# First token block of a mixture with plain products, its combined weights made one block later, and its weights taken through three stages

## The chip, the core and the metric

The kernel runs on one NeuronCore of a Trainium2 chip. The metric is the device time of one launch in microseconds (us). Five instruction streams run side by side and meet through semaphores: TensorE (PE: matrix products), ScalarE (ACT), VectorE (DVE), GpSimd (POOL) and SyncE (SP), which here does nothing but start DMA transfers between HBM and the on-chip memory SBUF. Products add up in PSUM, in banks of 512 float32 per partition. Each engine takes its instructions strictly in the order of the program, so an instruction that waits holds up all behind it.

## What is computed

```python
attn = softmax(q @ k.T / 8 + min(bias of s, 0), causal) @ v      # 4 x 8 heads, 576 tokens, 64 wide
x    = attn, heads side by side                                  # 2304 x 512
h    = x @ w_in ;  x  = (h * sigmoid(1.702 * h)) @ w_out         # first mixture, 512 -> 2048 -> 512
h2   = x @ w2_in;  r  = maximum(h2, 0)
out  = (s * r * r + b) @ w2_out                                  # second mixture, 512 -> 2048 -> 512
```

The weights arrive as 64-bit floats. The result must be as good as float32, so every factor is split into a high part that the fast matrix format holds exactly and a low rest, and every product is done three times (low times high, high times low, high times high).

## The kernel before

Attention and the first mixture run interleaved up to about 608 us of the trace. Then `first_whole` does the last 256 tokens of the first mixture on its own (to 648.6 us). The second mixture follows in `second`, for three blocks of 768 tokens (block 0, 1, 2).

A block is two halves of 384 tokens (N2). Its 16 hidden groups of 128 columns (f) are taken two at a time, in 8 steps p. Viewed over two token halves, two hidden groups and two halves of the 512 inputs, a step is a 2x2 by 2x2 block product, and `second` forms it from 7 products instead of 8, after Winograd: some factors are sums or differences of blocks. Each of the 7 slots of a step (`PRODUCTS`) has 6 matmuls of 128x384 into one of the PSUM sums p, q, r (L713), which ACT and DVE take out and add (`taken`, `added`), square, scale and split into g2 (`squared`, `affine`, `high`, `low`; the `low` of the odd group runs on POOL). Between the slots, `y_next` gives PE the output products of an earlier step from the list `todo`, 5 or 6 matmuls of 128x512 (L729) a slot.

The combined weights are made once, in block 0, one step ahead: `sums_of` forms four sums on POOL (L613), `parts_of` splits a part into high and low on ACT and DVE (L629, L630), 4 parts a step, and `hold` and `release` store them to HBM (`parts_d`). Blocks 1 and 2 read them back.

The raw weights come through a ring. `fetch_next` starts a transfer of 512 KB on SP into one of the `RING` buffers, 4 of them; it may run ahead of the last finished weight by that many. `sign_w` (ACT, L139), `merge_w` (two DVE instructions, L149 and L151) make float32 of the 64 bits, `split_w` (ACT L159, DVE L160) splits the output weights `wo`. `first_beside` deals these out by hand over the 7 slots. The order of every instruction on every engine is the order of the code here (`manual_schedule`).

```python
WHOLE, PARTS, SUMS, DIFFS = (0, 1, 11), (3, 4, 5, 8, 9, 10), 2, (6, 7)
EARLY2, RING = 4, (12, 13, 14, 15)
if k < EARLY2 or k < min(len(order), n_split[0] + len(RING)):    # fetch_next
```

Of the kernel before, what the change touches and what calls it, by code (L numbers as in the profile page):

```python
# [17 lines left out]
P = 128  # L18
# [17 lines left out]
HALF2, LAG2 = 384, 4  # L36
EARLY2, RING = 4, (12, 13, 14, 15)
WHOLE, PARTS, SUMS, DIFFS = (0, 1, 11), (3, 4, 5, 8, 9, 10), 2, (6, 7)
# [31 lines left out]
def fused_kernel(ctx: ExitStack, tc: tile.TileContext, qkT, vP, s, w1i, w1o, w2i, w2o, s2, b2, out):  # L70
# [473 lines left out]
    parts_d = dram.tile([NP, 4, P, 4 * W], F32, name="parts_d")  # L544
    tail1, early = ExitStack(), ExitStack()
# [3 lines left out]
    order = [("wi", f) for f in range(EARLY2)]  # L549
    for f in range(0, NF, 2):  # L550
        order += [("wi", f + k) for k in (EARLY2, EARLY2 + 1) if f + k < NF] + [("wo", f), ("wo", f + 1)]
    came, n_signed, joined, n_split = [], [0], [], [0]
    whole, wo2 = {}, {}

    def fetch_next():
        k = len(came)
        if k < EARLY2 or k < min(len(order), n_split[0] + len(RING)):
            tag, f = order[k]
            place = (early_pool, f"raw{k}", 1) if k < EARLY2 else (wp, f"wi{RING[k % len(RING)]}", 1)
            came.append(fetch_w(place, w2i if tag == "wi" else w2o, f))  # L560

    def sign_next():
        if n_signed[0] < len(came):
            sign_w(came[n_signed[0]])
            n_signed[0] += 1

    def merge_next():
        k = len(joined)
        if k < n_signed[0]:
            tag, f = order[k]  # L570
# [5 lines left out]
            joined.append(merge_w(came[k], to))  # L576

    def join_next():
        sign_next()
        merge_next()  # L580

    def split_next():

        if n_split[0] < len(joined):
            tag, f = order[n_split[0]]
            if tag == "wo":
                wo2[f] = split_w(joined[n_split[0]], "wo", f)
            n_split[0] += 1
# [14 lines left out]


# [11 lines left out]
    def parts_of(p, k, first):  # L616
# [5 lines left out]
        if not first:  # L622
            nc.sync.dma_start(flat, kept)
            return
        if k in (1, 2):
            src = sums[p][:, 2 * k - 2 : 2 * k].rearrange("p a n -> p (a n)")
        else:
            src = whole[p][:, 0, :] if k == 0 else whole[p][:, 1, W:]
# [4 lines left out]
    class Tokens:  # L633
# [25 lines left out]
        def split(self, kind, i, engine):  # L659
            t = self.d[i, kind] if len(kind) == 1 else self.at(i, int(kind[0]) - 1, int(kind[1]) - 1)  # L660
            x = self.x[kind, i] = xs_pool[0].tile([P, 2, N2], F32R, tag=f"x{kind}{i}", name="xs")
# [10 lines left out]
    def first_whole(ui, joins):  # L672
# [20 lines left out]
        for f in range(NF):  # L693
            for _ in h_item(ui, f, x, join_next if f in joins else None):
                pass
# [22 lines left out]
    y_sums = {}  # L718
    Y_OUT = (*RING, *WHOLE)
    y_tags = ["y4", "y0", "y1", "y2", "y3", None]  # L720

    def y_of(block, p, g2):

        def one(t, k):
            if p == 0 and k == 0:
                pool, tag = (psY, y_tags[t]) if y_tags[t] else (psM, "m")
                y_sums[t] = pool.tile([P, C], F32, tag=tag, name="py2", bufs=1 if y_tags[t] else 3)
            f, (a, b) = 1 - k // 3, ((1, 0), (0, 1), (0, 0))[k % 3]
            nc.tensor.matmul(  # L729
                y_sums[t], g2[f][:, a, t * P : (t + 1) * P], wo2[2 * p + f][:, b, :],  # L730
                start=(p == 0 and k == 0), stop=(p == NP - 1 and k == 5),
            )
            if p == NP - 1 and k == 5:
                y_out(block, t, y_sums[t])

        todo.extend((one, t, k) for t in range(T2) for k in range(6))

    def y_out(block, t, sums):
        row = block * 2 * N2 + t * P
        y = wp.tile([P, 2 * CM], F32, tag=f"wi{Y_OUT[t % (3 if block < N_BLOCKS - 1 else T2)]}", name="y2")[:, :C]  # L740
# [15 lines left out]
    def second(pool, gates, block, x, before, beside):  # L756
# [7 lines left out]
        def squared(c):  # L764
            nc.vector.scalar_tensor_tensor(out=c, in0=c, scalar=0.0, in1=c, op0=ALU.max, op1=ALU.mult)  # L765

        def affine(c):
            nc.scalar.activation(c, c, AF.Identity, scale=s_sb, bias=b_sb)  # L768

        def high(c, g2, f):  # L770
            g2[f] = gates().tile([P, 2, 2 * N2], F32R, tag="g2", name="g2", bufs=5)
            nc.scalar.activation(g2[f][:, 0, :], c, AF.Copy)  # L772

        def low(c, g2, f, engine):
            engine.tensor_tensor(g2[f][:, 1, :], c, f32(g2[f][:, 0, :]), ALU.subtract)  # L775

        for p in range(NP):
            step = block * NP + p
# [4 lines left out]
            for slot, (bank, _, _, _) in enumerate(PRODUCTS):  # L783
# [29 lines left out]
                if step == 0:  # L813
                    y_next(0 if slot == 6 else 2 * NC)
                elif step > 1 or slot >= LAG2:
                    y_next(6 if slot == 4 else 5)
            y_of(block, p, g2)
        return before

    def first_beside(p, slot):  # L820

        if p + 1 < NP:
            if p > 0 and slot == 0:
                sums_of(p + 1)
            k = {1: 0, 2: 1, 4: 2, 5: 3}.get(slot)
            if k is not None and (p > 0 or k > 1):
                parts_of(p + 1, k, True)
        if slot in (0, 1, 3, 4):
            sign_next()
        if slot in (1, 3, 5, 6):  # L830
            merge_next()
        if slot in (2, 3, 4, 6):
            split_next()
        fetch_next()
        fetch_next()
# [17 lines left out]

    with tc.manual_schedule(engines={PE, ACT, DVE, POOL, SP}):
        tokens = [Tokens(b * 2 * N2, (WHOLE[0], WHOLE[1], WHOLE[2], SUMS) if b else None) for b in range(N_BLOCKS)]
        x = tokens[0]
        X_FIRST = {
            6: lambda: (x.split("11", 0, L), x.split("11", 1, L), x.diff(0, 0, D)),
            7: lambda: (x.split("2", 0, D), x.split("1", 0, D), x.split("21", 0, L)),
            8: lambda: (x.diff(0, 1, D), x.split("3", 0, D), x.split("21", 1, L)),  # L860
            9: lambda: (x.split("4", 0, D), x.diff(1, 0, D), x.split("22", 0, L)),
            10: lambda: (x.split("2", 1, D), x.split("1", 1, D), x.split("22", 1, L)),
            11: lambda: x.diff(1, 1, D),
            12: lambda: (x.split("3", 1, D), x.split("4", 1, D)),
        }
        for f in first_whole(len(units) - 1, range(2, 2 + EARLY2)):
# [8 lines left out]
            split_next()  # L875
            release()
            if f == 1 + EARLY2:
# [4 lines left out]
            if f in (4, 7):  # L882
                sums_of(0 if f == 4 else 1)
            if f in (4, 5, 6, 8):
                parts_of(0, (4, 5, 6, 8).index(f), True)
            elif f in (11, 13):
                parts_of(1, (11, 13).index(f), True)
            if f >= RING[0]:
                fetch_next()
            if f in X_FIRST:  # L890
                X_FIRST[f]()
        tail1.close()
        pool = ctx.enter_context(tc.tile_pool(name="second", bufs=1, reuse_waits="tile"))
        before, gate_pool = [], []

        def gates():
            if not gate_pool:
                release(True)
                mixing.close()
                gate_pool.append(ctx.enter_context(tc.tile_pool(name="gates", bufs=1, side="right", reuse_waits="tile")))  # L900
            return gate_pool[0]
# [67 lines left out]
```

## Time and profile before

| | |
|---|---|
| time, median of 3 runs (lowest to highest) | 1065.11 us (1062.91 to 1065.68) |
| the profiled execution: its time, its span | 1064.85 us, 1063.1 us |
| PE busy | 1008.9 us (95%) |
| DVE busy | 681.5 us (64%) |
| ACT busy | 588.7 us (55%) |
| POOL busy | 365.2 us (34%) |
| mean granted clock of PE | 0.99 of 2.4 GHz |

The span is the stretch from the first to the last instruction that the profiler recorded. Busy shares are means over stages that differ: the page's slices show PE busy to nine tenths or more nearly everywhere, and to seven and eight tenths in a few slices between 664 and 771 us.

### The profile page before, as it was taken

How to read it: one execution, taken by the hardware profiler on the slowest of the kernel's cores; microseconds unless marked ns; L12 is line 12 of the kernel's file. 1: busy time of each engine (PE TensorE's matmuls, PEld its weight loads, DVE VectorE, ACT ScalarE, POOL GpSimd, SP SyncE). 2: the span in 40 equal slices, each digit the busy share in tenths (PEclk: the TensorE clock that was granted, in tenths of full speed). 3: DMA queues.
4: the chain of work that ended last, by engine and by line, in shares of the span. 5: the costliest groups of instructions: out<-in, count | busy, mean ns of one | idle time of the engine just before them, and what ended most of it. 6: DMA issues, size and time to landing. Idle time of an engine off the chain costs nothing. (4 is left out here: it accounts for less than half of the span.)

```text
span 1063.1 us, 17668 instructions
## 1 busy us (share of the span) xinstructions
PE 1008.9 (95%) x6264; PEld 921.1 (87%) x6264; DVE 681.5 (64%) x1453; ACT 588.7 (55%) x1322; POOL 365.2 (34%) x392
## 2 busy tenths in 40 slices
PE   5989999999999999999999999789899999999998
PEld 3459989999989999999999999677778888888887
DVE  5689877566467788878887476778884223642232
ACT  4788856646536646656656455645554342543332
POOL 2116535435335445435444282423321110310110
PEclk9998999999999999999999999999999999999999
DMA  6665432221042222222221146466754334342321
GB/s 193 197 222 185 123 99 56 64 81 44 11 133 71 69 92 70 83 90 82 77 86 51 46 183 208 134 221 210 238 216 160 130 119 158 138 173 96 139 70 60
DMA packets 51856, 129.58 MB, mean 122 GB/s; under 512 B 7068, under 2 KB 17432, under 8 KB 51768
## 3 DMA queue, kind: packets, MB, share of 16 engines
q1 hardware_dynamic: 51560, 128.32, 36.8%
q8 instruction: 50, 0.82, 0.3%
q14 instruction: 38, 0.31, 0.1%
q10 hardware_dynamic: 208, 0.13, 0.0%
HBM read 99.65 MB, written 24.71 MB: 117 GB/s over the span
## 5 line engine op out<-in xcount | busy, mean ns | idle before, releaser
L416 PE MATMUL ph<-xT,wi 128*128 128x320 f32 (+1 forms) x1536 | 245.8, 305 | 6.0 <-ACT xT L402 2.5
L729 PE MATMUL py<-wo,g 128*128 128x512 f32 x864 | 230.3, 398 | 11.0 <-DVE wo L160 11.0
L416 PEld LDWEIGHTS ph<-xT,wi 128*128 128x128 f32 x1536 | 216.6, 192 | 7.8 <-ACT xT L402 3.0
L456 PE MATMUL py<-g,wo 128*128 128x320 f32 (+1 forms) x1344 | 215.5, 304 | 0.0
L729 PEld LDWEIGHTS py<-wo,g 128*128 128x128 f32 x864 | 160.7, 189 | 39.1 <-DVE wo L160 13.1
L456 PEld LDWEIGHTS py<-g,wo 128*128 128x128 f32 x1344 | 188.2, 189 | 0.9
L443 POOL TENSOR_TENSOR g<-th,g 128x320 fp32r<-128x320 f32 (+1 forms) x128 | 111.7, 874 | 121.8 <-ACT g L442 120.1
L775 POOL TENSOR_TENSOR g<-odd,g 128x768 fp32r<-128x768 f32 x24 | 47.6, 1984 | 303.9 <-ACT g L772 303.9
L301 ACT ACTIVATE x<-x,m 64x64 f32<-64x64 f32 (+2 forms) x160 | 89.4, 559 | 99.5 <-DVE m L295 97.9
L713 PE MATMUL sum_p<-xs,part 128*128 128x384 f32 x576 | 119.7, 343 | 4.0 <-ACT e L759 4.0
L713 PEld LDWEIGHTS sum_p<-xs,part 128*128 128x128 f32 x576 | 105.1, 192 | 14.1 <-ACT e L759 6.5
L269 POOL TENSOR_TENSOR lo<-raw,hi 64x576 fp32r<-64x576 f32 (+1 forms) x56 | 68.2, 1218 | 123.3 <-PE ps L289 54.1
L295 DVE CUSTOM_DVE_ANT_0 x<-ps,mask 64x64 f32<-64x64 f32 (+2 forms) x160 | 68.1, 426 | 52.1 <-PE ps L289 50.2
L327 PE MATMUL pst<-ident,x 128*128 128x128 f32 (+2 forms) x480 | 85.9, 287 | 10.0 <-DVE ph L336 8.6
L759 ACT ACTIVATE e<-sum_p 128x384 f32<-128x384 f32 x72 | 35.2, 489 | 97.5 <-PE sum_p L713 97.5
L116 POOL TENSOR_SCALAR x<-x,tot 64x64 f32<-64x64 f32 (+1 forms) x96 | 49.4, 522 | 93.0 <-DVE tot L306 54.7
L333 ACT ACTIVATE ph<-pst 64x256 fp32r<-64x256 f32 (+2 forms) x144 | 67.1, 474 | 20.7 <-PE pst L327 19.3
L442 ACT ACTIVATE g<-th 128x320 fp32r<-128x320 f32 (+1 forms) x128 | 56.4, 441 | 40.1 <-DVE th L438 39.6
L327 PEld LDWEIGHTS pst<-ident,x 128*128 128x128 f32 (+2 forms) x480 | 54.9, 136 | 24.9 <-DVE ph L336 13.2
L437 ACT ACTIVATE th<-ph 128x320 f32<-128x320 f32 (+1 forms) x128 | 51.5, 402 | 35.5 <-PE ph L416 33.6
L438 DVE SCALAR_TENSOR_TENSOR th<-th,ph 128x320 f32<-128x320 f32 (+1 forms) x128 | 57.3, 448 | 20.9 <-ACT th L437 19.8
L118 DVE TENSOR_SCALAR hi<-raw 128x832 fp32r<-128x832 f32 (+1 forms) x48 | 69.0, 1437 | 2.3 <-DMA raw<-qkT 2.1
(100 smaller groups left out, 1607.9 us busy)
## 6 DMA issues: line engine op xcount, KB each, us to landing
part<-parts_d SPq DMA_DIRECT2D x48, 512.0 KB
raw<-qkT SPq DMA_DIRECT2D x32, 416.0 KB
parts_d<-part SPq DMA_DIRECT2D x24, 512.0 KB
pair<-w1o SPq DMA_DIRECT2D x16, 512.0 KB
pair<-w1i SPq DMA_DIRECT2D x16, 512.0 KB
pair<-w2i SPq DMA_DIRECT2D x16, 512.0 KB
pair<-w2o SPq DMA_DIRECT2D x16, 512.0 KB
raw<-qkT SPq DMA_DIRECT2D x24, 320.0 KB
```

Of the source, the lines that this page charges most:

```text
L118: nc.vector.tensor_scalar(out=out, in0=in_, scalar1=scale, scalar2=None, op0=ALU.mult)
L269: nc.gpsimd.tensor_tensor(lo[:D, kc], raw[:D, kc], f32(hi[:D, kc]), ALU.subtract)
L295: nc.vector.tensor_tensor_reduce(out=x[:w, j0:j1], in0=ps[:w, : j1 - j0], in1=mask[:w, WIDE - a0 + j0 : WIDE - a0 + j1], scale=-1.0 / ROOT ...
L301: nc.scalar.activation(x[:w, :a1], x[:w, :a1], AF.Exp, bias=least, scale=-1.0, accum_out=tot[:w, c : c + 1])
L327: nc.tensor.transpose(ps[: j1 - j0, at : at + a1 - a0], t["x"][c][: a1 - a0, j0:j1], ident[: a1 - a0, : a1 - a0])
L333: nc.scalar.activation(t["ph"][:rows, base:end], ps[:rows, :m], AF.Copy)
L416: nc.tensor.matmul(ph[:, :n], wi[f][:, a, cc * P : (cc + 1) * P], x[cc][:, b, :n], start=(k == 0), stop=(k == 3 * NC - 1),)
L438: nc.vector.scalar_tensor_tensor(out=th[:, :n], in0=th[:, :n], scalar=1.0, in1=ph[:, :n], op0=ALU.add, op1=ALU.mult)
L443: nc.gpsimd.tensor_tensor(g[:, 1, :n], th[:, :n], f32(g[:, 0, :n]), ALU.subtract)
L456: nc.tensor.matmul(py[:, :n], wo[f][:, a, wc], g_t[ui, f][:, b, :n], start=(k == 0), stop=(k == 3 * G - 1))
L713: nc.tensor.matmul(ps[:, :N2], w[:, a, c0 : c0 + P], x[kind, k // 3][:, b, :], start=(first and k == 0), stop=(k == 5), skip_group_check=n ...
L729: nc.tensor.matmul(y_sums[t], g2[f][:, a, t * P : (t + 1) * P], wo2[2 * p + f][:, b, :], start=(p == 0 and k == 0), stop=(p == NP - 1 and ...
```

## The change

Block 0 leaves `second` and gets a loop of its own, `halves`. It goes through 16 groups f times 2 token halves, 32 slots, 4 to a step of two groups. A slot has 12 matmuls of 128x384 with the split weights of one group themselves (`wi2`, the plain product, no combinations), then up to 8 output products; ACT takes the sum out with one copy, and after the second half the group is squared, scaled and split. The output products of a group are listed as soon as the group is done, not two groups at a time.

The raw ring gets 8 buffers. `weight_next`, once a slot, does three things for three different weights: it merges the next one, splits the one merged a slot before, and signs the one after. The split of an input weight is used by `halves` directly; as the first and the fourth part of the Winograd form are just pieces of it, those are stored to `parts_d` from there, and the merged float32 weights are stored too (`whole_d`).

Block 1 now makes the other two parts: it reads the merged weights back (`fetch_whole`), forms the sums on POOL and splits two parts a step, storing them for block 2; the other two it reads. The splits of block 0's tokens need 8 pieces and no differences; those of block 1 move to the last steps of block 0 (`X_SECOND`).

```diff
-EARLY2, RING = 4, (12, 13, 14, 15)
-WHOLE, PARTS, SUMS, DIFFS = (0, 1, 11), (3, 4, 5, 8, 9, 10), 2, (6, 7)
+EARLY2, RING = 4, (8, 9, 10, 11, 12, 13, 14, 15)
+WHOLE, SPLIT = (0, 1), (2, 3, 4, 5, 6, 7)
+PARTS, SUMS, DIFFS = (12, 8, 9, 3, 10, 4), 2, (6, 7)
...
+    def weight_next():
+
+        k = n_done[0]
+        ready = k < len(merged)
+        if len(merged) < n_signed[0]:
...
+            merged.append(merge_w(came[len(merged)], to))
+            if tag == "wi" and f % 2:
+                hold(1, whole_d[f // 2], whole[f // 2].rearrange("p f n -> p (f n)"))
+        if ready:
+            tag, f = order[k]
             if tag == "wo":
-                wo2[f] = split_w(joined[n_split[0]], "wo", f)
-            n_split[0] += 1
+                wo2[f] = split_w(merged[k], "wo", f)
+            else:
+                split_wi(f)
+            n_done[0] += 1
+        if n_signed[0] < len(came):
+            sign_w(came[n_signed[0]])
+            n_signed[0] += 1
...
+    def fetch_whole(p):
+        whole[p] = wp.tile([P, 2, CM], F32, tag=f"wi{WHOLE[0]}", name="whole")
+        nc.sync.dma_start(whole[p].rearrange("p f n -> p (f n)"), whole_d[p])
...
-        if not first:
+        if not first or k in (0, 3):
             nc.sync.dma_start(flat, kept)
             return
...
+        for s in range(4 * NP):
+            p, f, n = s // 4, s // 2, s % 2
...
+            for k in range(3 * NC):
+                cc, (a, b) = k // 3, ((1, 0), (0, 1), (0, 0))[k % 3]
+                nc.tensor.matmul(
+                    ps[:, :N2], wi2[f][:, a, cc * P : (cc + 1) * P], x[f"{cc // 2 + 1}{n + 1}", cc % 2][:, b, :],
+                    start=(k == 0), stop=(k == 3 * NC - 1),
+                )
+            beside(p, s % 4)
+            if s != 2:
+                y_next(6 * NC if s < 2 else 8)
+            nc.scalar.activation(c[:, n * N2 : (n + 1) * N2], ps[:, :N2], AF.Copy)
+            if n == 0:
+                continue
+            squared(c)
+            affine(c)
+            high(c, g2, f % 2)
+            low(c, g2, f % 2, nc.gpsimd if f % 2 and f > 1 else nc.vector)
+            if f < NF - 2:
+                y_of(0, (f,), g2)
...
+            if slot < 2 or 2 * p + slot + EARLY2 < NF:
+                weight_next()
+            release()
+            fetch_next()
+            fetch_next()
...
+                if block == 1 and p + 1 < NP:
+                    if slot == 1:
+                        sums_of(p + 1)
+                        if p + 2 < NP:
+                            fetch_whole(p + 2)
```

The order of the instructions shows three places. In the rows, `pair` is a raw weight, `pair<-pair` its signing, `wo` and `wi` split weights, `whole` a merged one, `part` a part of the Winograd form, `e`, `even`, `odd` and `c` sums taken out of PSUM. First ACT, from the first slot of a step in the middle of block 0, before:

```order
L759 ACTIVATE e<-sum_p 128x384
L768 ACTIVATE even<-even,b_sb,s_sb 128x768
L139 ACTIVATE pair<-pair 128x512
L772 ACTIVATE g_9221<-even 128x768
L629 ACTIVATE part<-whole 128x512
L139 ACTIVATE pair<-pair 128x512
L759 ACTIVATE e<-sum_p 128x384
L629 ACTIVATE part<-sums 128x512
L159 ACTIVATE wo_9246<-pair 128x512
L139 ACTIVATE pair<-pair 128x512
L759 ACTIVATE e<-sum_p 128x384
L629 ACTIVATE part<-sums 128x512
```

and the same place now, ACT from the first slot of a step in `halves`:

```order
L161 ACTIVATE wo_9063<-pair 128x512
L141 ACTIVATE pair<-pair 128x512
L810 ACTIVATE c<-ph_9048 128x384
L161 ACTIVATE wo_9095<-pair 128x512
L141 ACTIVATE pair<-pair 128x512
L810 ACTIVATE c<-ph_9079 128x384
L783 ACTIVATE c<-c,b_sb,s_sb 128x768
L787 ACTIVATE g_9112<-c 128x768
L596 ACTIVATE wi_9131<-whole 128x512
L141 ACTIVATE pair<-pair 128x512
L810 ACTIVATE c<-ph_9116 128x384
```

Every slot now has the same three instructions (split, sign, take out), with the chain of a finished group behind the second. Second SP, the transfers of one step of block 0, before:

```order
L128 DMA pair<-w2o 128x1024
L601 DMA parts_d<-part 128x1024
L601 DMA parts_d<-part 128x512
L128 DMA pair<-w2o 128x1024
L128 DMA pair<-w2i 128x1024
L601 DMA parts_d<-part 128x1024
L128 DMA pair<-w2i 128x1024
L601 DMA parts_d<-part 128x1024
```

and now:

```order
L130 DMA pair<-w2i 128x1024
L614 DMA whole_d<-whole 128x1024
L614 DMA parts_d<-wi_8995 128x1024
L130 DMA pair<-w2i 128x1024
L614 DMA parts_d<-wi_9025 128x2x256
L130 DMA pair<-w2o 128x1024 x2
```

The four raw weights stay, and three stores take the place of four. Third PE in the middle of block 0, two slots before:

```order
L713 MATMUL sum_p<-xs,part 128x384 x6
L729 MATMUL py_9028<-wo_9176,g_9221 128x512 x2
L729 MATMUL py_9056<-wo_9246,g_9170 128x512 x3
L713 MATMUL sum_q<-xs,part 128x384 x6
L729 MATMUL py_9056<-wo_9176,g_9221 128x512 x3
L729 MATMUL py_9080<-wo_9246,g_9170 128x512 x2
```

and two slots now:

```order
L803 MATMUL ph_9252<-xs,wi_8883 128x384 x12
L753 MATMUL py_8940<-wo_9063,g_9112 128x512 x2
L753 MATMUL py_8891<-wo_9095,g_9180 128x512 x3
L753 MATMUL py_8895<-wo_9095,g_9180 128x512 x3
L803 MATMUL ph_9282<-xs,wi_8883 128x384 x12
L753 MATMUL py_8899<-wo_9095,g_9180 128x512 x3
L753 MATMUL py_8932<-wo_9095,g_9180 128x512 x3
L753 MATMUL py_8936<-wo_9095,g_9180 128x512 x2
```

A slot has grown from 6 + 5 matmuls to 12 + 8, and a step has 4 slots in place of 7.

## Rows read from the trace of the kernel before

**Rows 1.** Windows by stage: length, busy time (instructions) of each engine, clock, DMA share, GB/s.

```profile
core 0: us, PE busy (x) PEld busy (x) DVE busy (x) ACT busy (x) POOL busy (x), PEclk, DMA share, GB/s
608.17:648.56 40.39, 40.05 (x338) 39.84 (x337) 29.06 (x44) 21.04 (x52) 26.33 (x28) 1.00 0.54 194
648.56:794.31 145.75, 128.21 (x618) 110.64 (x617) 113.55 (x161) 81.81 (x147) 44.74 (x37) 0.96 0.60 202
794.31:920.28 125.97, 125.97 (x625) 112.89 (x624) 49.30 (x70) 52.13 (x82) 19.64 (x12) 1.00 0.41 142
920.28:1046.26 125.98, 125.98 (x626) 112.88 (x624) 41.50 (x59) 49.81 (x74) 16.54 (x9) 1.00 0.32 115
```

**Rows 2.** Timeline of PE in block 0: start, length, instruction, [idle before, releaser].

```profile
712.65 1.43 PE L729 MATMUL py<-wo,g 128*128 128x512 f32 x5 [1.83 <-DVE wo L160]
713.92 1.21 PE L713 MATMUL sum_p<-xs,part 128*128 128x384 f32 x6
714.96 1.33 PE L729 MATMUL py<-wo,g 128*128 128x512 f32 x5
716.13 1.21 PE L713 MATMUL sum_r<-xs,part 128*128 128x384 f32 x6
...
731.13 2.30 PE L729 MATMUL py<-wo,g 128*128 128x512 f32 x5 [1.85 <-DVE wo L160]
```

**Rows 3.** Timeline of PE: block 1's first product, and the end of block 2.

```profile
794.31 1.21 PE L713 MATMUL sum_p<-xs,part 128*128 128x384 f32 x6
...
1045.09 14.39 PE L729 MATMUL py<-wo,g 128*128 128x512 f32 x61
```

**Rows 4.** Waits in block 0: who waited for whom, us in total, times, longest.

```profile
ACT pair L139 <- DMA pair<-w2o: 34.7, 12, 6.0
...
PE py L729 <- DVE wo L160: 11.0, 6, 2.5
...
PE sum_p L713 <- ACT e L759: 4.0, 2, 2.5
```

**Rows 5.** Timeline of SP's queue: a raw weight's transfer is started.

```profile
712.62 0.33 SPq L128 DMA_DIRECT2D pair<-w2o  x1
```

**Rows 6.** Timeline of ACT: the signing of that weight.

```profile
716.49 0.67 ACT L139 ACTIVATE pair<-pair 128x512 f32<-128x512 f32 x1 [3.94 <-DMA pair<-w2o]
```

**Rows 7.** Timeline of DVE in the same step: split low parts and merges, twice each.

```profile
704.36 2.15 DVE L160 TENSOR_TENSOR wo<-pair,wo 128x512 fp32r<-128x512 f32 x1
...
708.41 0.96 DVE L149 TENSOR_SCALAR pair<-pair 128x512 uint32<-128x512 uint32 x1
709.41 1.11 DVE L151 SCALAR_TENSOR_TENSOR whole<-pair 128x512 uint32<-128x512 uint32 x1
...
711.91 0.68 DVE L160 TENSOR_TENSOR wo<-pair,wo 128x512 fp32r<-128x512 f32 x1
712.52 0.41 DVE L149 TENSOR_SCALAR pair<-pair 128x512 uint32<-128x512 uint32 x1
712.97 0.69 DVE L151 SCALAR_TENSOR_TENSOR whole<-pair 128x512 uint32<-128x512 uint32 x1
```

**Rows 8.** Timeline of POOL: block 0's low part and last sum, then block 1's low part.

```profile
703.81 2.16 POOL L775 TENSOR_TENSOR g<-odd,g 128x768 fp32r<-128x768 f32 x1 [12.52 <-ACT g L772]
...
709.05 0.92 POOL L613 TENSOR_TENSOR sums<-whole,sums 128x256 f32<-128x256 f32 x1
...
810.44 1.92 POOL L775 TENSOR_TENSOR g<-odd,g 128x768 fp32r<-128x768 f32 x1 [11.01 <-ACT g L772]
```

**Rows 9.** Groups of block 0 by shape: count, busy us, mean ns, idle before.

```profile
L759 ACT ACTIVATE e<-sum_p 128x384 f32<-128x384 f32 x24 | 11.5, 481 | 5.3 <-PE sum_p L713 5.3
L765 DVE SCALAR_TENSOR_TENSOR odd<-odd 128x768 f32<-128x768 f32 x8 | 7.6, 951 | 0.0
L768 ACT ACTIVATE odd<-odd,b_sb,s_sb 128x768 f32<-128x768 f32 x7 | 7.2, 1030 | 18.3 <-DVE odd L765 18.3
L775 DVE TENSOR_TENSOR g<-even,g 128x768 fp32r<-128x768 f32 x7 | 6.6, 945 | 0.0
L772 ACT ACTIVATE g<-odd 128x768 fp32r<-128x768 f32 x7 | 5.9, 847 | 0.2
```

More of the change, by code (lines that the diff above doesn't have):

```diff
@@ L754, in y_out, with squared, affine, high @@
             release(True)
-    def second(pool, gates, block, x, before, beside):
+    def squared(c):
+        nc.vector.scalar_tensor_tensor(out=c, in0=c, scalar=0.0, in1=c, op0=ALU.max, op1=ALU.mult)
+    def affine(c):
+        nc.scalar.activation(c, c, AF.Identity, scale=s_sb, bias=b_sb)
+    def high(c, g2, f):
+        g2[f] = gates().tile([P, 2, 2 * N2], F32R, tag="g2", name="g2", bufs=5)
+        nc.scalar.activation(g2[f][:, 0, :], c, AF.Copy)
+    def low(c, g2, f, engine):
+        engine.tensor_tensor(g2[f][:, 1, :], c, f32(g2[f][:, 0, :]), ALU.subtract)
+    def halves(pool, x, beside):
+        for s in range(4 * NP):
+            p, f, n = s // 4, s // 2, s % 2
+            if n == 0:
+                c = pool.tile([P, 2 * N2], F32, tag="c", name="c", bufs=3)
+                if f % 2 == 0:
+                    g2 = [None, None]
+            ps = psM.tile([P, 512], F32, tag="m", name="ph2")
+            for k in range(3 * NC):
[8 more added lines that the diff above has]
+            nc.scalar.activation(c[:, n * N2 : (n + 1) * N2], ps[:, :N2], AF.Copy)
+            if n == 0:
+                continue
[5 more added lines that the diff above has]
+                y_of(0, (f,), g2)
+            elif f == NF - 1:
+                y_of(0, (f, f - 1), g2)
+    def second(pool, block, x, before, beside):
         def taken(t, bank):
@@ L812, in second @@
                 beside(p, slot)
[L813 to L817, printed above, removed]
-        return before
[L820 to L835, printed above, removed]
+                y_next(6 if slot == 4 else 5)
+            y_of(block, (2 * p + 1, 2 * p), g2)
+        return before
     D, L = nc.vector, nc.gpsimd
@@ L881, in fused_kernel @@
                 x.fetch(NC - 1)
[L882 to L887, printed above, removed]
             if f >= RING[0]:
                 fetch_next()
-            if f in X_FIRST:
-                X_FIRST[f]()
+            if f in (8, 9, 10, 11):
+                for i in range(2):
+                    x.split(("11", "21", "12", "22")[f - 8], i, D)
@@ L892, in fused_kernel, with first_beside @@
         tail1.close()
         pool = ctx.enter_context(tc.tile_pool(name="second", bufs=1, reuse_waits="tile"))
[L894 to L901, printed above, removed]
+        before = []
+        def first_beside(p, slot):
+            if slot < 2 or 2 * p + slot + EARLY2 < NF:
+                weight_next()
+            release()
+            fetch_next()
+            fetch_next()
+            if p == NP - 2:
+                tokens[1].fetch((0, 2, 1, 3)[slot])
+                if slot == 0:
+                    fetch_whole(0)
+            if p == NP - 1:
+                if slot == 0:
+                    sums_of(0)
+                    fetch_whole(1)
+                parts_of(0, slot, True)
+            if (p, slot) in X_SECOND:
+                X_SECOND[p, slot](tokens[1])
@@ L916, in beside @@
                     X_WORK[p - NP, slot](after)
-                if block and (p, slot) in X_WORK:
+                if block > 1 and (p, slot) in X_WORK:
                     X_WORK[p, slot](x)
-            second(pool, gates, block, x.x, before, beside)
+                if block == 1 and (p + NP, slot) in X_SECOND:
+                    X_SECOND[p + NP, slot](x)
+            second(pool, block, x.x, before, beside)
         nc.scalar.activation(before[0], before[0], AF.Identity, scale=s_sb, bias=b_sb)
```

128 lines of the change are left out of this document (61 added, 67 removed).

## The prediction, made before the changed kernel had run

> **What bounds the kernel now.** I read the slices of the page first: PE is the engine that sets the time, and its only thin stretch lies behind 648 us. So I cut the trace into windows at the stage boundaries [rows 1]. In the stage ahead, PE is busy 40.05 of 40.39 us; blocks 1 and 2 take 125.97 and 125.98 us and PE is never idle in them. Block 0 takes 145.75 us for the same number of sum products, PE is idle 17.5 us of it, and its mean granted clock is 0.96 where the other blocks have 1.00.
>
> What should block 0 cost? In PE's timeline six sum products run from 713.92 to 714.96 (0.174 us each), five output products from 714.96 to 716.13 (0.234) [rows 2]. A block has 7 x 6 x 8 = 336 of the first and 6 x 6 x 8 = 288 of the second: 58.5 + 67.4 = 125.9, which is what blocks 1 and 2 take. At the end 61 output products stand in one row, 5 of the last slot and 56 left over [rows 3]. Blocks 1 and 2 do as many a step as they list, so 56 were also left over at the end of block 0, which did 232 of its own, and 48 of the first mixture at 40.05 / 338 = 0.1185. Block 0's work is 58.5 + 54.3 + 5.7 = 118.5 us; 145.75 - 118.5 = **27.2 us are lost**.
>
> Where? The stall of PE comes back once a step: 1.83 us before an output product at 712.65, 1.85 before the one at 731.13, 18.5 us later, where a step of blocks 1 and 2 is 15.75 [rows 1, 2]. The list of waits names the split of an output weight on DVE, 11.0 us in 6 times, and ACT's signing of raw weights, which waited 34.7 us for their transfers [rows 4]. One weight shows the circle. DVE's split low part at 711.91 frees a ring buffer [rows 7]; SP starts the next transfer at 712.62 [rows 5]; ACT, after 3.94 us idle, signs it at 716.49 [rows 6], so a transfer takes 3.9 us, and with four buffers it starts only when its weight is about to be wanted. All that ACT has behind the signing waits too, then DVE, which has to catch up at its slowest: a low part takes 2.15 us beside POOL's instruction at 703.81 and 0.68 away from POOL, a merge 0.96 + 1.11 or 0.41 + 0.69 [rows 7, 8]. Then the output weight is late for PE. Five output products took 1.43 us after one stall and 2.30 after another [rows 2]: the second ran at the lower level of the clock. Part of the 27.2 us is such slow work.
>
> **The change, part by part.** *Products.* Block 0 does 32 x 12 = 384 sum products in place of 336: 48 x 0.174 = **8.4 us more**. Output products stay: `y_next` gives 24 + 24 of the first mixture, then 29 x 8 = 232, and 56 are left over as before. Block 0 without a wait is 66.8 + 54.3 + 5.7 = 126.8 us, 18.9 less than now.
>
> *The ring.* Eight buffers let a transfer start eight weights ahead of the last split, and signing comes two slots ahead of its split. That leaves six slots. A slot is 12 x 0.174 + 8 x 0.234 = 3.96 us, so 23.8 us for a transfer that takes 3.9. ACT's wait for transfers should go. Traffic does not speak against it: a step of block 0 moved 2048 KB of weights and 1792 KB of parts in 18.5 us (212 GB/s); now it is 2048 + 512 (merged) + 768 (two parts) = 3328 KB in 15.85 us, 215 GB/s, near the 202 GB/s of the window, where the DMA engines were busy 0.60 [rows 1].
>
> *ACT and DVE in block 0.* This is what could take the stall's place, since a group passes from ACT to DVE and back with the weights' work queued ahead of it. I followed one step. First group: ACT split 0.67 (taken like the signing, same shape), DVE low 0.68, merge 1.10, low 0.68, square 0.95, ACT scale 1.03 and high part 0.85 [rows 6, 7, 9]: 5.96. Second group: DVE must first make the first group's low part, 0.95, then merge, low, merge, low, square, and ACT's two: 7.34. Together 13.3 us against PE's 15.85; the copies out of PSUM (0.48) and the signings fit beside DVE's work. That is the lower bound. The upper one takes every low part at 2.15 and every merge at 2.07, as beside POOL [rows 7]: 22.1. I stay near the lower: POOL now has one instruction of 2.16 us a step [rows 8] where it had sums as well (44.74 us in the window [rows 1]), so about one low part a step collides: 13.3 + 1.5 = 14.8, hidden behind PE.
> The low part at 704.36 started 0.55 us after POOL's and ended 0.54 after POOL's end [rows 7, 8]. The Trainium skill (SBUF — State Buffer, "Who interferes with whom") has VectorE and GpSimd share a port pair that the first holds for its whole instruction; the trace agrees, and by that rule a step's collisions cost at most POOL's 2.16, so 15.5, still hidden: the sum would be the same.
>
> *Start and end of block 0.* The first group's gate has no backlog of output products to cover it: after the copies of the first mixture it needs take-out, square, scale, high, low, 0.48 + 0.95 + 1.03 + 0.85 + 0.95 = 4.3 us, while PE has two slots of 12 products, 4.2 us. Some tenths are lost. At the end, differences and splits of block 1's tokens queue on ACT and DVE before the last group's gate, and block 1's third slot needs ACT to have taken its first sum. Below, nothing is lost; above, the like wait, PE for ACT's take-out, came to 4.0 us, 2.5 the longest [rows 4]. I take **2 us** for both ends.
>
> *Block 1* gets per step four sums on POOL (0.92 the last one; I take 1 each), two splits (0.67 ACT, 0.68 DVE) and 512 KB in. Its DVE goes from 49.30 / 8 = 6.2 to 7.5 us, POOL from 2.5 to 6.5, ACT from 6.5 to 7.8, all of 15.75 [rows 1]: hidden. One new wait has something behind it: SP's `fetch_whole` waits until POOL has read the old tile, and the next step's first part is queued behind. POOL's low part starts 0.4 us into the step (810.44 against 794.31 + 15.75 [rows 3, 8]), so the sums end at 0.4 + 1.9 + 4 = 6.3. Two transfers, even one after the other, land at 14.2, before the 15.75 at which the part is wanted. Nothing, as long as transfers keep 3.9 us.
>
> Sum against the profiled execution: 1064.85 - 27.2 + 8.4 + 2 = **1048 us**. The median of the runs, 1065.11, is 0.26 higher, which changes nothing.
>
> **The rivals.** *ACT and DVE set block 0's pace.* For it: DVE was busy 113.55 us of block 0, 14.2 a step, and the loop has only 1.0 us to spare after one collision. Against it: that 14.2 holds the collisions with sums that are gone, and the adding out of PSUM. Halfway between the bounds, 17.7, it costs 1.85 us in each of the five steps in which all four slots have a weight, 9 us: 1057; a little over the edge, 1051 to 1054.
>
> *Block 1 pays.* If a transfer took the longest wait in the list, 6.0 us [rows 4], the part would land at 18.3, 2.6 late, in seven steps: 18 us, 1066, no gain. Against it: block 1 moved 142 GB/s, and gets less than block 0 has. The edge is a transfer of 4.7 us; partly, 1052 to 1060.
>
> *Slower.* DVE meets POOL at every instruction: 22.1 a step, five times 6.2 over PE, 31 us: 1079. It decides from a loop of 15.85 + 18.9 / 5 = 19.6 us. Against it: POOL would have to be busy most of a step. Or the change doesn't do what it says, the ring still starting each transfer when it is wanted: then the extra products come on top, 1073. Against it: six slots lie between.
>
> **How the numbers follow.** No wait worth naming, 1046 to 1051: 0.66, and 1048 is its middle. Pace of ACT and DVE, 1051 to 1057: 0.16. Block 1 pays: 0.09, a fourth of it up to no gain. The two slower cases together: 0.06. Gains that go by ways I don't see: 0.03. A measurement of this kernel can't tell less than 0.3% (3.2 us) from no change. Faster 0.89, the same 0.04, slower 0.07. The range from 1045.5 (no loss at either end, less the spread of runs) to 1057 leaves out the slower cases and the worst of block 1.
>
> **What would show it.** Right: block 0 from 648.6 to about 777 us; no wait of ACT for raw weights; PE's stalls short and only near the first gate and at the change of blocks; a clock of 1.00 throughout; blocks 1 and 2 at 126 us. Wrong: ACT still waiting for transfers (the ring); PE waiting for DVE's or POOL's low part of a gate, or for ACT's take-out, in the middle of block 0 (the loop); PE waiting for a part, or a block 1 over 128 us (the price moved); DVE low parts at 2 us where POOL is idle (the collision isn't POOL's).

## The result and the profile after

The changed kernel takes **1046.18 us** (median of 4 runs, 1045.72 to 1047.03) against 1064.28 us of the kernel before in the same session (4 runs, 1062.91 to 1065.68): a ratio of 0.9831, 95% interval 0.9814 to 0.9848, 18 us faster. The forecast was 1048.0 us, with a range of 1045.5 to 1057. The profiled execution took 1045.72 us with a span of 1043.8.

The same four stages as [rows 1], windows by stage of the changed kernel:

```profile
core 0: us, PE busy (x) PEld busy (x) DVE busy (x) ACT busy (x) POOL busy (x), PEclk, DMA share, GB/s
605.84:645.72 39.88, 39.88 (x339) 39.88 (x338) 23.94 (x43) 22.31 (x52) 13.57 (x15) 1.00 0.75 256
645.72:773.49 127.77, 127.04 (x666) 115.82 (x665) 83.01 (x118) 75.11 (x125) 16.37 (x11) 1.00 0.54 182
773.49:901.06 127.57, 126.36 (x624) 112.94 (x625) 58.96 (x88) 58.68 (x98) 43.27 (x39) 1.00 0.47 170
901.06:1027.05 125.99, 125.99 (x626) 112.89 (x624) 41.52 (x59) 49.81 (x74) 16.57 (x9) 1.00 0.33 115
```

Block 0 went from 145.75 to 127.77 us, 1.0 above the 126.8 of its products; its clock is 1.00. Block 1 is 1.6 longer, the stage ahead 0.5 shorter, block 2 the same: 16.9 us less in all. The rest of the 19.3 us between the two spans lies before 608 us, where the changed kernel's trace is 2.33 us earlier, though the change touches nothing there. In the 14 profiled executions of this study block 0 began anywhere from 645.1 to 650.5 us, and most of that spread lies ahead of the edits. What moves that stretch was not looked for. So below the length of a stage in the trace decides, and the median beside it.

PE's timeline answers to [rows 2, 3]: the first gate, a steady pair of slots, the change of blocks, the end.

```profile
655.60 4.34 PE L803 MATMUL ph<-xs,wi 128*128 128x384 f32 x24
660.54 2.13 PE L753 MATMUL py<-wo,g 128*128 128x512 f32 x8 [0.61 <-DVE g L790]
...
690.19 2.25 PE L803 MATMUL ph<-xs,wi 128*128 128x384 f32 x12
692.27 2.03 PE L753 MATMUL py<-wo,g 128*128 128x512 f32 x8
694.14 2.25 PE L803 MATMUL ph<-xs,wi 128*128 128x384 f32 x12
...
779.42 1.31 PE L727 MATMUL sum_p<-xs,part 128*128 128x384 f32 x6 [1.21 <-ACT e L825]
...
1025.88 14.39 PE L753 MATMUL py<-wo,g 128*128 128x512 f32 x61
```

A slot takes 3.95 us (694.14 - 690.19), the forecast 3.96. The two waits shown are all that PE's list of waits holds from block 0 on; the rows of ACT waiting for raw weights [rows 4] are gone. Two more looks at one step, ACT first and then DVE and POOL, answer to [rows 6 to 8]:

```profile
692.47 0.63 ACT L596 ACTIVATE wi<-whole 128x512 fp32r<-128x512 f32 x1 [2.75 <-PE ph L803]
...
700.38 0.49 ACT L810 ACTIVATE c<-ph 128x384 f32<-128x384 f32 x1 [0.78 <-PE ph L803]
```

```profile
697.58 1.88 DVE L162 TENSOR_TENSOR wo<-pair,wo 128x512 fp32r<-128x512 f32 x1 [1.47 <-ACT wo L161]
...
700.50 0.68 DVE L162 TENSOR_TENSOR wo<-pair,wo 128x512 fp32r<-128x512 f32 x1
```

```profile
697.06 1.85 POOL L790 TENSOR_TENSOR g<-c,g 128x768 fp32r<-128x768 f32 x1 [13.88 <-ACT g L787]
```

Now ACT waits for PE, 2.75 and 0.78 us in a step of 15.81: I take this as the margin of the loop between ACT and DVE. One instruction of DVE a step meets POOL (1.88 beside 0.68).

### The profile page after: what moved, and what is told of

Its sections match the earlier page's. It is cut to its first block, busy times and chain, and to the rows that moved or that the text cites. A ratio compares the mean times of both kernels' runs of the same rounds, so it can differ in the third digit from the quotient of the medians.

```text
span 1043.8 us, 17713 instructions
## 1 busy us (share of the span) xinstructions
PE 1007.1 (96%) x6312; PEld 925.2 (89%) x6312; DVE 655.6 (63%) x1426; ACT 589.9 (57%) x1316; POOL 346.8 (33%) x381
## 4 chain that ended last, share of the span: by engine, by line
PE 78%; DVE 11%; ACT 5%; DMA 3%; issue 2%; SPq 1%; POOL 0%; DVEq 0%; ACTq 0%; POOLq 0%
PE py L753 18%; PE py L458 15%; PE ph L418 14%; PE sum_p L727 6%; PE ph L803 5%; PE ps L291 5%; PE pst L329 4%; PE sum_r L727 3%; DVE hi L120 3%; PE po L356 3%; PE py L694 2%; PE sum_q L727 2%; DVE x L297 1%; ACT x L303 1%; DMA pair<-w1i 1%
## 5 line engine op out<-in xcount | busy, mean ns | idle before, releaser
L753 PE MATMUL py<-wo,g 128*128 128x512 f32 x864 | 224.5, 395 | 0.6 <-DVE g L790 0.6
L445 POOL TENSOR_TENSOR g<-th,g 128x320 fp32r<-128x320 f32 (+1 forms) x128 | 112.8, 883 | 133.5 <-ACT g L444 124.4
L790 POOL TENSOR_TENSOR g<-odd,g 128x768 fp32r<-128x768 f32 x16 | 30.4, 1899 | 183.6 <-ACT g L787 183.6
L727 PE MATMUL sum_p<-xs,part 128*128 128x384 f32 x384 | 78.0, 337 | 1.3 <-ACT e L825 1.2
L335 ACT ACTIVATE ph<-pst 64x256 fp32r<-64x256 f32 (+2 forms) x144 | 67.1, 473 | 20.7 <-PE pst L329 19.1
L727 PEld LDWEIGHTS sum_p<-xs,part 128*128 128x128 f32 x384 | 69.0, 188 | 7.5 <-ACT e L825 1.6
L803 PE MATMUL ph<-xs,wi 128*128 128x384 f32 x384 | 71.8, 335 | 0.0
L825 ACT ACTIVATE e<-sum_p 128x384 f32<-128x384 f32 x48 | 23.6, 491 | 84.9 <-PE sum_p L727 84.9
```

The costliest lines, as they stand in the source:

```text
L335: nc.scalar.activation(t["ph"][:rows, base:end], ps[:rows, :m], AF.Copy)
L445: nc.gpsimd.tensor_tensor(g[:, 1, :n], th[:, :n], f32(g[:, 0, :n]), ALU.subtract)
L727: nc.tensor.matmul(ps[:, :N2], w[:, a, c0 : c0 + P], x[kind, k // 3][:, b, :], start=(first and k == 0), stop=(k == 5), skip_group_check=n ...
L753: nc.tensor.matmul(y_sums[t], g2[f % 2][:, a, t * P : (t + 1) * P], wo2[f][:, b, :], start=(first and k == 0), stop=end)
L803: nc.tensor.matmul(ps[:, :N2], wi2[f][:, a, cc * P : (cc + 1) * P], x[f"{cc // 2 + 1}{n + 1}", cc % 2][:, b, :], start=(k == 0), stop=(k = ...
```

## The experiments

All ratios are to the kernel before in the same session. Each run was measured four times except the one-slot kernel (ten).

**Was it the ring?** Two more buffers for the kernel before, and nothing else:

```diff
-EARLY2, RING = 4, (12, 13, 14, 15)
+EARLY2, RING = 4, (12, 13, 14, 15, 6, 7)
```

> The kernel before with one edit: the ring of raw weights has six buffers in place of four (two more, taken from the buffers of the output staging); block 0 keeps the Winograd form, its 48 fewer products and its combined weights. My theory, that block 0 lost its 27.2 us because a transfer started only when its weight was about to be wanted: two more buffers start it two weights earlier, about half a step or 8 us, against a transfer of 3.9 us, so ACT's wait for raw weights (34.7 us) falls under 10 us, and block 0 from 145.75 to between 122 and 134 us; the time is 1041 to 1053 us, and since it has no extra products (8.4 us) it could beat the changed kernel. The rival, that the combined weights set the pace (ACT and DVE with 14.2 us of DVE work a step, sums on POOL beside it): ACT's waits for raw weights shrink, but PE then waits for the split of output weights or for the combined parts all the same, block 0 stays over 138 us, and the time over 1057 us.

1049.83 us, ratio 0.9883 (0.9857 to 0.9909). ACT's waits for raw weights fell from 34.7 us to 0.3, yet block 0 still took 133.5 us: its window, what is left of those waits, and rows of PE's timeline.

```profile
645.33:778.86 133.53, 123.11 (x619) 109.24 (x618) 113.74 (x161) 82.16 (x147) 44.85 (x37) 0.97 0.67 233
```

```profile
ACT pair L139 <- DMA pair<-w2o: 0.3, 1, 0.3
```

```profile
663.14 1.32 PE L713 MATMUL sum_p<-xs,part 128*128 128x384 f32 x6 [2.46 <-ACT e L759]
...
671.04 2.50 PE L729 MATMUL py<-wo,g 128*128 128x512 f32 x5 [2.57 <-DVE wo L160]
...
689.60 1.43 PE L729 MATMUL py<-wo,g 128*128 128x512 f32 x5 [0.51 <-DVE wo L160]
...
706.24 1.43 PE L729 MATMUL py<-wo,g 128*128 128x512 f32 x5 [0.66 <-DVE wo L160]
```

The ring was worth 12.2 us of the 27.2: PE was idle 7.1 us less, and its own products took 5.1 us less (busy 123.11 in place of 128.21 us). What is left are waits in the second step (2.46, 1.30 and 2.57 us idle, and slow products behind the last: five took 2.50 us, with a granted clock of 0.50, the lower level, from 671 to 674 us), one of 0.51 to 0.66 us in each of the next five steps, and 0.99 us at the change of blocks. So both theories were half right.

**How many buffers does the changed kernel need?** Its ring cut to four, `(8, 9, 10, 11)`, and to three, `(8, 9, 10)`:

> The changed kernel with a ring of four buffers in place of eight. By my theory the distance between the start of a transfer and its signing is what counts: with four buffers and signing two slots ahead of the split, two slots of 3.96 us are left, 7.9 us for a transfer of 3.9 us: the time stays within 1 us of the changed kernel's 1046.2 us, and ACT has no wait for raw weights over 0.5 us in block 0. The rival, that it takes the eight buffers (transfers are bunched, or SP starts them late behind stores that wait): ACT waits for transfers again, block 0 takes 3 to 15 us more, 1049 to 1061 us.

> The changed kernel with a ring of three buffers. By my theory one slot of 3.96 us is left for a transfer of 3.9 us and the 0.7 us until SP starts it: too little by about 0.7 us a weight, some 28 weights through the ring. ACT's waits for raw weights come back in the list of waits (10 to 40 us in all), and, as a signing is two slots ahead of its split, part of it is taken up by the loop's slack: block 0 takes 2 to 20 us more than with eight buffers, 1048 to 1066 us. The rival, that the number of buffers was not what cost the kernel before its time (the combined weights, or the three things done to one weight in one slot, were): no wait of ACT over 1 us in total, and 1045.5 to 1047 us.

Four: 1046.42 us, block 0 127.87, no wait for a transfer. Three: 1054.93 us, block 0 134.52, and the list of waits of block 0 has them back:

```profile
ACT pair L141 <- DMA pair<-w2i: 20.9, 10, 3.7
...
ACT pair L141 <- DMA pair<-w2o: 7.9, 3, 3.9
```

Two slots ahead are enough for a transfer of 3.9 us, one is not. Eight buffers buy nothing over four.

**Are the three stages needed?** All three things done to one weight in one slot, and the two ways between; in short, what `weight_next` does in a slot, k being the weight that is split in it:

```diff
-after          merge(k+1); split(k);   sign(k+2)
+one slot       sign(k);    merge(k);   split(k)
+sign ahead     merge(k);   split(k);   sign(k+1)
+split later    split(k);   sign(k+1);  merge(k+1)
```

> The changed kernel with eight buffers, but a weight is signed, merged and split all in one slot, as it was before, and not in three slots one after another. If the eight buffers alone remove the loss, nothing changes but the order: the loop of ACT and DVE gets one more way there and back (signing 0.67, merge 1.1, high part 0.67, low part 0.68, each waiting for the one before), some 15.7 us in my reckoning against 15.85 of PE, so 0 to 3 us more than the changed kernel: 1046 to 1049 us. If the stagger is what removes it (the rival), PE waits for the split of a weight (input or output) several times a step and the time is 1052 to 1065 us, with no wait of ACT for a raw weight.

> The changed kernel with two stages: a weight is signed one slot ahead, then merged and split in one slot. The run with everything in one slot took 1061.9 us, since ACT's take-out of a sum stands behind a split that waits for DVE's merge, which waits for ACT's signing, and PE waits for the take-out. By this theory one of the two ways between the engines is still ahead of the take-out (merge on DVE, then split on ACT), so part of the loss stays: 1048 to 1056 us, with ACT's splits waiting for DVE's merges and PE's product for ACT's take-out in the list of waits. A rival, that only the signing behind the gate's high part costs (DVE's merge waited 2.2 us for it once a step): within 1 us of the changed kernel's 1046.2 us.

> The changed kernel with the other two stages: a weight is signed and merged in one slot and split one slot later. By the theory of the take-out nothing on ACT waits for DVE's work on the same weight ahead of a take-out any more, since the split finds its weight merged a slot before, so PE doesn't wait: 1046 to 1048 us. By the rival, that every way between the two engines lengthens the loop by the same, this costs about half of the 15.7 us that three stages gain over one: 1051 to 1057 us, as DVE's merge still waits for ACT's signing behind the gate's high part and all of DVE behind it is late.

One slot: **1061.86 us**, ratio 0.9986 (0.9974 to 0.9998), nearly all of the gain gone with eight buffers in place and no wait for a raw weight. Sign ahead: 1055.94. Split later: 1051.52. Windows of block 0 of the three, in this order, one fence each:

```profile
649.50:790.96 141.46, 130.32 (x667) 114.93 (x665) 84.97 (x122) 77.77 (x127) 15.88 (x11) 1.00 0.51 165
```

```profile
647.39:783.93 136.54, 128.74 (x667) 115.32 (x665) 85.33 (x120) 76.29 (x126) 16.36 (x11) 1.00 0.52 171
```

```profile
647.81:779.55 131.74, 128.69 (x666) 115.25 (x665) 82.61 (x118) 74.95 (x125) 15.95 (x11) 1.00 0.51 176
```

DVE and ACT are busy nearly as long as in the changed kernel (83 and 75 us); only the order differs. ACT's timeline of the one-slot kernel, with one row of DVE's and two of PE's, shows what the order does:

```profile
707.42 0.85 ACT L782 ACTIVATE g<-c 128x768 fp32r<-128x768 f32 x1
708.17 0.65 ACT L141 ACTIVATE pair<-pair 128x512 f32<-128x512 f32 x1
710.77 0.66 ACT L161 ACTIVATE wo<-pair 128x512 fp32r<-128x512 f32 x1 [1.95 <-DVE pair L153]
711.33 0.48 ACT L805 ACTIVATE c<-ph 128x384 f32<-128x384 f32 x1
```

```profile
708.85 1.88 DVE L153 SCALAR_TENSOR_TENSOR pair<-pair 128x512 uint32<-128x512 uint32 x1 [2.19 <-ACT pair L141]
```

```profile
711.86 2.35 PE L798 MATMUL ph<-xs,wi 128*128 128x384 f32 x12 [1.08 <-ACT c L805]
...
730.06 2.35 PE L798 MATMUL ph<-xs,wi 128*128 128x384 f32 x12 [1.15 <-ACT c L805]
```

The signing stands behind the gate's high part; DVE's merge (708.85, 1.88 beside POOL) waits for it, ACT's split for the merge, the take-out stands behind the split, and PE's next product began at 711.86 after 1.08 us idle. PE's waits of this kind repeat every 18.20 us (711.86, 730.06), against 15.81 with three stages. Two stages lie between: with signing ahead 17.48 (700.88, 718.36), with splitting later 17.12:

```profile
714.26 2.35 PE L800 MATMUL ph<-xs,wi 128*128 128x384 f32 x12 [0.76 <-ACT c L807]
...
731.38 2.35 PE L800 MATMUL ph<-xs,wi 128*128 128x384 f32 x12 [0.79 <-ACT c L807]
```

```profile
ACT wo L161 <- DVE pair L153: 11.9, 8, 2.2
```

My theory of the take-out alone (with splitting later, a split finds its weight merged a slot before, so nothing waits) fell: that kernel lost 4.0 us of block 0. The merge, behind a signing of its own slot, came out late, so that ACT's splits of output weights still waited for it, 11.9 us in 8 times (25.0 in 16 with one slot), and PE still waited for take-outs. The losses of the two hand-overs, 8.8 and 4.0, add up to 12.8 of the 13.7 us of both: each lengthens the loop, as the rival said, though not by the same.

**Did the combined weights have to go?** Sums and two splits of steps 3 to 7 back in block 0; then the sums alone, as an extra that nobody reads. Both have a ring of five buffers:

```diff
+            if slot == 3 and p + 3 < NP:
+                sums_of(p + 3, 13)
+            if slot < 2 and 0 < p and p + 2 < NP:
+                parts_of(p + 2, 1 + slot, True, 14 + slot)
```

> The changed kernel, with the sums and the two split combined parts of steps 3 to 7 made in block 0 again, one step after their weights, and stored; block 1 reads them. Ring of five buffers. Per step of block 0 POOL gets four sums, 4.1 us, ACT two splits, 1.3 us, DVE two low parts, 1.4 us alone and 4 us beside POOL. If moving the combined weights is a needed part of the gain: ACT's and DVE's chain of 13.3 to 14 us a step goes to 16 to 18 us, PE waits for a take-out or a split in five steps, 1 to 10 us more, 1047 to 1056 us. If it isn't (the ring and the stages do it all): 1045.5 to 1047 us, with block 1 a little shorter or the same.

> The changed kernel (ring of five) with the four sums a step on POOL in five steps of block 0 as an extra, with no splits from them; nobody reads them, and block 1 makes its own as before. With two splits a step beside them it took 9 us more (1055.3 us). If the meetings of DVE with POOL are what that cost: 5 to 9 us more than the changed kernel, 1051 to 1055 us, with DVE's low parts and merges at 1 to 2 us while POOL is busy. If the two extra splits in ACT's and DVE's chain cost it: at most 1.5 us more, 1046 to 1048 us. By the bounds of the prediction, 1 us for each sum at the most and 2 us of slack in a step, five steps cost 0 to 10 us.

1055.27 us and 1049.39 us; the second lies between its two expectations. Windows, the first kernel's blocks 0 and 1, then the second's block 0, and two rows of PE's timeline of the first:

```profile
645.69:780.20 134.51, 128.52 (x666) 115.51 (x665) 98.08 (x128) 79.49 (x135) 37.02 (x31) 1.00 0.63 216
780.20:907.78 127.58, 126.34 (x625) 112.90 (x625) 54.89 (x78) 54.08 (x88) 25.75 (x19) 1.00 0.42 149
```

```profile
647.32:777.11 129.79, 127.96 (x666) 115.51 (x664) 92.20 (x118) 74.44 (x125) 37.10 (x31) 1.00 0.55 184
```

```profile
705.65 2.38 PE L804 MATMUL ph<-xs,wi 128*128 128x384 f32 x12 [0.86 <-ACT c L811]
...
722.98 2.38 PE L804 MATMUL ph<-xs,wi 128*128 128x384 f32 x12 [1.22 <-ACT c L811]
```

With sums and splits block 0 takes 6.7 us more, with the sums alone 2.0. (By the medians it is 9.1 and 3.2, by the ratios, each to its own session, some 8 and 2.6; in the second kernel's profiled execution block 0 also began 1.6 us later than the changed kernel's.) So the move was needed: the loop's margin of 2.75 + 0.78 us takes up most of the meetings with POOL, but not the two splits as well, and a step then takes 17.33 us (PE's waits at 705.65 and 722.98). Block 1 is as long without five of its seven steps of extra work (127.58) as with them (127.57): there it is hidden.

**What holds the Winograd form?** The kernel before with six buffers, and on top of that: weights one place earlier; POOL's sums left out, so that two parts are split from the merged weights as they are and the values differ; weights earlier and the sums on DVE.

```diff
+        if (p, slot) == (2, 5):
+            sign_next()
+        if (p, slot) == (3, 0):
+            merge_next()
+        if (p, slot) == (3, 1):
+            split_next()
...
+            if p < 1:
+                nc.gpsimd.tensor_tensor(to, a, b, op)
...
+            (nc.vector if p > 1 else nc.gpsimd).tensor_tensor(to, a, b, op)
```

> The kernel before with a ring of six buffers, and from the third step on every weight signed, merged and split one place earlier (one more weight is pushed through at once there). With six buffers alone (1049.8 us) block 0 still took 133.5 us, 15 over its 118.5 us of work, and PE waited 0.65 us for the split of an output weight in each of five steps; a step took 16.64 us in place of 15.75. If the place of the split in the order is the cause, five steps lose their 0.9 us each: 3 to 5 us less, 1045 to 1047 us. If ACT's and DVE's work sets that pace (14.2 us of DVE a step and its ways to and from ACT), another instruction is late in its place and the time stays within 1.5 us of 1049.8.

> The kernel before with a ring of six buffers, in which POOL's four sums a step are left out from the second step of weights on: two combined parts are then split from the merged weights as they are, so the values differ, and the number of splits, stores and products stays. If DVE's meetings with POOL's sums are what holds block 0 at 133.5 us: about four meetings a step of 0.4 to 1 us each go, the waits for the split of an output weight (0.65 us in five steps) go, and the time is 1044 to 1047 us. If the number of splits and the late first gate of the Winograd form hold it, 1048.5 to 1050 us. In both cases about 6 us of idle PE in the second step (two waits for ACT's take-out, one for an output weight) stay, since nothing there changes.

> The Winograd form with a ring of six buffers and the weights one place earlier, and the four sums of each later step on DVE in place of POOL. Without the sums, block 0 took 125.9 us and DVE was busy 105.5 us of it; with them on POOL, 133.5 and 113.7 us, or 129.2 us with the weights one place earlier. A 128x256 instruction of DVE took 0.42 us, so four a step for six steps add some 10 us of DVE, more than the 8 us by which the meetings with POOL stretched its instructions. If DVE's total work is what sets block 0, it stays at 129 us or gets longer, 1046.5 to 1051 us. If only the place counts (POOL's sums met the first merge and the low part behind it, ahead of the split that PE waits for), sums in slot 0 on DVE lie just there too, and nothing is gained either: 1047 to 1050 us. Under 1045 us, with a block 0 under 127.5 us, would say that a meeting with POOL costs DVE more than doing the work itself.

1049.50, 1042.64 and 1049.17 us. Windows of block 0 in this order, and two rows of PE's timeline of the first:

```profile
647.81:777.05 129.24, 122.10 (x618) 109.10 (x617) 113.87 (x161) 82.01 (x147) 43.88 (x37) 0.99 0.69 240
```

```profile
646.33:772.24 125.91, 121.18 (x618) 109.14 (x617) 105.49 (x161) 81.45 (x145) 20.55 (x12) 0.99 0.72 246
```

```profile
650.47:779.83 129.36, 122.73 (x619) 108.90 (x617) 114.20 (x185) 82.10 (x147) 19.99 (x13) 0.99 0.69 240
```

```profile
673.50 1.43 PE L729 MATMUL py<-wo,g 128*128 128x512 f32 x5 [2.54 <-DVE wo L160]
...
690.13 1.43 PE L729 MATMUL py<-wo,g 128*128 128x512 f32 x5 [0.65 <-DVE wo L160]
```

Without the sums the old form takes 125.9 us, 7.6 less. DVE is busy 8.25 us less with the same 161 instructions; as no row in the list of waits of the kernel with six buffers has an engine waiting for a sum, it is the meetings that are gone. PE has no wait at all in its middle steps; what stays is 2.48 and 1.15 us in the second step and 1.04 at the end. The expectation missed on both counts: it had 1044 to 1047 us and some 6 us of waits in the second step. (One of the four runs took 1048.06 us, the others 1042.26 to 1042.78.)

The earlier place of the weights takes away four of the five waits near 0.65 us and brings a new one of 0.56. Block 0 is 4.3 us shorter, but not all of that is the edit's. Between the two rows shown, before the order differs, the edited kernel takes 16.63 us, and the one with six buffers takes 18.56 between the same places (671.04 to 689.60), with a clock of 1.00 against 0.88. From there to the end of block 0 it is 86.92 against 89.26 us: 2.3 us are left for the edit. The median hardly moved and missed the 1045 to 1047 us expected, and the intervals of the two ratios overlap, so the total of this pair stays unclear. The sums on DVE gain nothing over POOL in block 0 (129.4 against 129.2): four instructions of 0.42 us cost DVE about what the meetings cost.

**A better version.** Four buffers, and in the free ones block 1's tokens one step earlier, with their differences and splits:

```diff
-EARLY2, RING = 4, (8, 9, 10, 11, 12, 13, 14, 15)
+EARLY2, RING = 4, (8, 9, 10, 12)
...
-        (7, 3): lambda x: (x.split("21", 0, D), x.split("21", 1, D), x.split("1", 1, D), x.split("4", 0, D)),
+        (7, 3): lambda x: (x.split("21", 0, D), x.split("21", 1, D)),
```

> A version that might beat the changed kernel: its ring has four buffers (which cost nothing), so the tokens of block 1 are fetched one step earlier, and their differences and most of their splits that don't wait for block 0's tokens move from the last step of block 0 into the one before, where DVE was busy 8.4 of 15.8 us. At the change of blocks PE waited 1.21 us for ACT's take-out of the first sum, which stood behind the gate of block 0's last group, and that behind DVE's splits (square at 776.10, 2.4 us after PE had done the group's product). If this is the cause: that wait goes, block 0 and block 1 together lose 1 to 1.6 us, 1044.6 to 1045.3 us. If the gate itself is what is late (its own chain of 4 us), 1046 us as before; if the new work in the step before makes the group's gates late there, over 1047 us.

1044.86 us, ratio 0.9813 (0.9790 to 0.9835). Its blocks 0 and 1:

```profile
647.14:775.15 128.01, 127.05 (x667) 115.86 (x665) 86.02 (x123) 77.58 (x129) 16.65 (x11) 1.00 0.57 191
775.15:901.19 126.04, 126.04 (x624) 112.95 (x625) 56.15 (x82) 56.69 (x94) 43.30 (x39) 1.00 0.48 172
```

The wait of 1.21 us at the change of blocks is gone, and the two blocks take 254.05 us in place of 255.34, as expected. In the total the intervals of the two kernels overlap, so that it is the fastest version is shown by its stages, not by its time.

## Why the prediction held, step by step

- *27.2 us are lost in block 0.* Right as a size: 1.0 us is left above the products. PE was idle for 17.5 of the 27.2; for the other 9.7 its products took longer, as at 731.13 [rows 2], where its granted clock was 0.56 up to 733.23. **Wrong as to the cause.** I followed one weight through the ring and let its circle stand for all. The runs, one profiled execution each, split the loss: 12.2 the ring (six buffers), 7.6 DVE's meetings with POOL's sums (sums left out), and 7.4 the rest, 125.9 against 118.5. Of this rest 4.7 are waits of PE in the second step and at the change of blocks, and for 2.7 PE is busy longer (its clock was 0.93 up to the end of the second step's last wait). The change removes all three: ring and distance, sums to block 1, and a gate after 2 slots of 12 products, with output products listed by the group. So the sum came out although its reason covers less than half of the loss; for the rest that was luck.

  Two things stay open. No run takes the third part away alone: that the plain form does it is read from the waits that are missing. And no run varies one more thing that the change brings: six weights are split when block 0 begins, where the kernel before had four merged. The one-slot kernel has these six too and still took 141.46 us, so alone they don't carry the gain.
- *Six slots for a transfer of 3.9 us.* Right; the edge lies between one slot (three buffers, 6.7 us more) and two.
- *48 products, 8.4 us.* Confirmed by the slot of 3.95 us and block 0 at 127.77. But not all of it is a price against the old form, which lost 7.4 us even with ring and sums out of the way, 125.9 us in all.
- *ACT and DVE, 13.3 to 14.8 us a step.* Hidden, as forecast; ACT's 3.5 us of waiting for PE put the loop at some 12.3 (15.81 - 3.5, an estimate). I had not said that this rests on the three stages: with one the same work takes 18.2 us a step. The rival "ACT and DVE set block 0's pace" was closer than its chance of 0.16 said: one hand-over more in a slot brings it about.
- *Start and end of block 0, 2 us.* 0.61 at the first gate; the wait foretold in block 1's third slot, for ACT's take-out, is the row at 779.42. With block 1's 1.6 us and block 0's 1.0 the ends cost 2.6.
- *Block 1's extra work: nothing.* Right: the same length with and without five of its seven steps.
- *The collision.* The low part beside POOL took 1.88 in place of 0.68 and ended 0.55 us after POOL's. The Trainium skill (SBUF — State Buffer, "Who interferes with whom") has one of the two wait for the other's instruction; one meeting a step agrees. Behind four sums in a row the stretch was less than POOL's time: 9.2 us for 20.7.

The forecast was 1.8 us high. Its stages were not: it gave the two blocks 128.8 + 126.0, they took 127.8 + 127.6. The difference is the stretch ahead of block 0, which shifts from execution to execution.

## What to carry to other kernels

A weight that passes ACT, DVE, ACT, DVE within one slot of the loop puts each hand-over in front of whatever stands behind it in the two queues; dealing the stages of different weights into one slot costs nothing but a buffer or two, and was worth 13.7 us here with the work unchanged. A long list of waits for transfers names one cause, not the only one: take it away alone (two more buffers) before the whole loss is put down to it. Judge a small change by the stage it touches when the stretch ahead of it scatters by more than the change.

## What the runs showed of the hardware that was not expected

POOL's instructions slow DVE by less than their own length when both have several in a row. DVE's timeline of the kernel with the sums as an extra, beside four sums on POOL from 696.07 to 700.29, of which the first and the last are shown:

```profile
696.44 0.97 DVE L151 TENSOR_SCALAR pair<-pair 128x512 uint32<-128x512 uint32 x1
697.52 1.04 DVE L153 SCALAR_TENSOR_TENSOR pair<-pair 128x512 uint32<-128x512 uint32 x1
698.48 1.22 DVE L597 TENSOR_TENSOR wi<-whole,wi 128x512 fp32r<-128x512 f32 x1
699.62 1.49 DVE L780 SCALAR_TENSOR_TENSOR c<-c 128x768 f32<-128x768 f32 x1
```

```profile
696.07 1.06 POOL L630 TENSOR_TENSOR sums<-whole 128x256 f32<-128x256 f32 x1 [7.40 <-DVE whole L153]
...
699.11 1.18 POOL L630 TENSOR_TENSOR sums<-whole,sums 128x256 f32<-128x256 f32 x1
```

Away from POOL these take 0.42, 0.69, 0.69 and 0.95 us, so DVE paid 2.0 us for 4.2 us of POOL. And moving such work from POOL to DVE was no gain: 4 x 0.42 us of DVE against about 1.4 us a step of stretching (8.25 us in six steps with sums, by DVE's 113.74 and 105.49).
